# First block's layers as whole float32 products, weight splits made later and weight conversion moved behind each step's work

## Chip, cores and metric

The kernel runs on one core of a Trainium2 chip. The metric is the device time of one execution in microseconds (us). Before the change the median of three runs is 1035.82 us, the lowest 1035.16 us.

## What is computed

An attention-like recurrence (wkv) over 768 steps, for 4 sequences and 8 heads of 48 channels, gives 3072 tokens of 384 values. Two layers follow:

```python
h = x @ w_in                                  # 384 -> 2048
x = (h * clip(h + 3, 0, 6) / 6) @ w_out       # 2048 -> 384
xn = x / sqrt(mean(x * x) + 1e-6) * rms_g
g = xn @ w_gate                               # 384 -> 1536
x = (g / (1 + exp(-g)) * (xn @ w_val)) @ w_out2   # 1536 -> 384
```

Inputs are float32; the weights of the two layers come as 64-bit words (float64) and are turned into float32 on the core.

## The kernel before

**Blocks.** The 768 steps are cut in six chunks (c = 0 to 5) of 128 steps; a chunk of all four sequences is a block of 512 tokens. Attention is worked in 24 jobs (chunk, sequence). The first layer takes block after block, and attention jobs of later blocks run between its matmuls. Then comes the second layer (`gps`, `vps` and `o` products), block after block, in which only matmuls and their follow-up remain.

**Steps.** The first layer is a list of 101 steps, each for one slice f (of 16) of the 2048 hidden values. A step (`ff1`) makes `hps` in three k-tiles (`emit_h`), then relu6 on ScalarE and VectorE (`emit_act`), then the split of the result; two steps later `ff2` adds the slice's part into three accumulators `o` (`emit_out`). In block 0 the first five slices are done in two halves of 256 tokens (steps 0 to 4 and 5 to 9), since the jobs of sequences 2 and 3 are not ready yet; steps 10 to 20 take 512 tokens each. Block 1 has eight slices in halves, from step 21.

**Products.** A float32 operand is split in two float32r parts, high and low; a product of a 128x128 weight tile is three matmuls (`PASS`: high-high, high-low, low-high). Hence nine matmuls for a step's `hps` and nine for its `o`. Splits: weights in `Weight.parts` (high on ScalarE, low on GpSimd), hidden values in `emit_split` (the same), attention output in `split_y0` (ScalarE, VectorE) for block 0.

**Weights.** Each weight tile (128x768, 64 bits each) is loaded to `raw`, then `scale` (ScalarE, tile `mag`, one buffer), `bits` (three VectorE instructions L143, L144, L146 into tile `x`), then `parts`. The 16 tiles of the first layer are converted during block 0, the 18 of the second one (`wb`) during block 5 and the first eight steps of the second layer. What a step does before its matmuls, between and behind them is in the lists `before`, `between` and `behind`; `pin` fixes each engine's order to that of the code. Every engine works its own instructions in that order.

**Norm.** When a block's last `o` is done, `Norm` copies the three accumulators away (two on ScalarE, L378, one on VectorE, L376); the next block's first `o` waits for these copies. The rest of the norm is spread over later steps.

Of the kernel before, what the change touches and what calls it, by code (L numbers as in the profile page):

```python
# [9 lines left out]
F32 = mybir.dt.float32  # L10
# [12 lines left out]
DM = H * D  # L23
# [6 lines left out]
NB = 3 * F2 // 2  # L30
NX = 6
NE = 10
# [4 lines left out]
def kernel(  # L37
# [84 lines left out]


    class Weight:
        def __init__(self, src, dst):
            self.src, self.dst = src, dst

# [8 lines left out]
        def scale(self):  # L136
            self.mag = st_p.tile([128, 2 * DM], F32, tag="mag", name="mag", bufs=1)
# [20 lines left out]
    class Job:  # L158
# [172 lines left out]

        def split_y0(self):
            xt = self.xt()
            nc.scalar.activation(out=xt[:, :, 0, :], in_=self.yps, func=AF.Copy)
            nc.vector.tensor_tensor(
                out=xt[:, :, 1, :], in0=self.yps, in1=xt[:, :, 0, :].bitcast(F32), op=ALU.subtract)

# [7 lines left out]

    def emit_act(ps, n):
        a = rg_p.tile([128, n], F32, tag="a", name="a", bufs=2)
        nc.scalar.activation(out=a, in_=ps, func=AF.Relu, scale=1.0 / 6.0, bias=half)  # L348
        nc.vector.scalar_tensor_tensor(out=a, in0=a, scalar=1.0, in1=ps, op0=ALU.min, op1=ALU.mult)  # L349
        return a  # L350

# [5 lines left out]

    def emit_out(acc, slot, g, first, last, cols, **kw):
        for m in range(KT):
            for j, (l, r) in enumerate(PASS):  # L360
                nc.tensor.matmul(  # L361
                    acc[m][:, cols], slot[:, l, m * 128:(m + 1) * 128], g[:, r, :],
                    start=(first and j == 0), stop=(last and j == 2), **kw)

# [4 lines left out]
    class Norm:  # L369
# [41 lines left out]
    jobs = [Job(c, b) for c in range(NC_) for b in range(B)]  # L411
    wa = [Weight(wa_d[f], None) for f in range(F1)]
    whole, halves = slice(0, TOK), (slice(0, HT), slice(HT, TOK))
# [65 lines left out]
    def ff1(c, f, cols):  # L479
        n = cols.stop - cols.start  # L480
        ps = ps_h.tile([128, n], F32, tag="h", name="hps")
        emit_h(wpair[f][:, 0], xts[c][:, :, :, cols], ps)
        a = emit_act(ps, n)
        g = emit_split(a, n)
        todo.append(lambda: ff2(c, f, cols, g))

    def ff2(c, f, cols, g):
        nonlocal acc
        lagged = LAGS[c] > 0
        if f == 0 and cols.start == 0:  # L490
            acc = new_acc()
            if lagged:
                for m in range(KT):
                    nc.tensor.matmul(
                        acc[m], zero, wpair[0].rearrange("p a l n -> p (a l n)")[:, 0:TOK], start=True, stop=False)
        last = f == F1 - 1
        emit_out(acc, wpair[f][:, 1], g, f == 0 and not lagged, last, cols)
        if last:
            norms[c] = Norm(c, acc)
# [17 lines left out]

    j0.load("w", "rk")
    j1.load("w")
    for t, s in ((iperm, iperm_d), (mask, mask_d)):  # L520
        nc.sync.dma_start(out=t, in_=s)
    nc.vector.memset(uc, 0.0)
    for i in range(2):
        nc.sync.dma_start(
            out=uc[64 * i:64 * i + D, :, i], in_=u_d.rearrange("o (p i d) -> i d (o p)", p=NP, i=2)[i])
    j1.load("rk")
    j0.load("v")
# [17 lines left out]
    for t in st_all:  # L545
        nc.gpsimd.memset(t, 0.0)
    nc.scalar.activation(out=zero, in_=st_all[3][:, 0:128], func=AF.Copy)
    for f in range(W1):
        wa[f].dst = wpair[f]
    run((j0.scans, j0.pairs, j0.pe_bonus, j0.muls, j0.fill, j0.pe_a, j1.scans, j1.pairs, j1.pe_bonus, j1.muls))  # L550
    run((j0.choose, j1.fill, j1.pe_a, j0.pe_y0, wa[0].scale, wa[0].bits, j1.choose, j1.pe_y0))
    run((j0.split_y0, wa[0].parts, wa[1].scale, wa[1].bits, j1.split_y0, j2.scans, wa[1].parts))
    pin()


    for n, (c, f, cols) in enumerate(steps):
# [8 lines left out]
        if n == first[NC_ - 1]:  # L565
            actx.close()
            st_p = pool(ctx, "st2", 2, side="left", reuse_waits="tile")
            b_p = pool(ctx, "bp", 2, side="left", reuse_waits="tile")
# [3 lines left out]
            wb = [Weight(wb_d[i], extra[i] if i < NX else wpair[i - NX]) for i in range(NB)]  # L572
            wb[0].load()
            wb[1].load()
        run(before[n])
        if c == NC_ - 1:
# [16 lines left out]
        run(behind[n])  # L593
        pin()
# [26 lines left out]
    for c in range(NC_):  # L621
        for f in range(F2):
            if c == 0:
                if f < NB - NE:
                    wb[NE + f].scale()
# [17 lines left out]
            if len(todo) > 2:  # L643
                todo.pop(0)()
            if c == 0 and 2 <= f < 2 + len(NORM):
                x = NORM[f - 2]
                getattr(norms[NC_ - 1], x[0])(*x[1:])
            if c + 1 < NC_:
# [91 lines left out]
```

## Time and profile before

| what | value |
|---|---|
| median of three runs | 1035.82 us |
| the profiled execution, its own time | 1035.39 us |
| its span, first to last instruction | 1033.6 us |
| TensorE (PE) busy | 972.1 us, 94% |
| VectorE (DVE) busy | 482.4 us, 47% |
| ScalarE (ACT) busy | 405.5 us, 39% |
| GpSimd (POOL) busy | 441.8 us, 43% |
| loads to `raw` (768 KB each), issue to landing, median | 4.3 us |
| mean granted TensorE clock | 0.969 of full speed |

The profile is of one execution. Each engine works through its own instructions in order; where an instruction waits, the profile says for which other engine. Shares of the whole span hide that stretches differ, so the stretches are read one by one. The span of a PE row is modelled at its end; the distance between starts is what a stream of matmuls costs. PEld rows are the weight loads that go with the matmuls. PEclk is the granted clock of TensorE as a share of 2.4 GHz; 0.5 is the lower of its two levels, 1.2 GHz.

### The profile page before, as it was taken

What the parts mean: (1) busy time and instruction counts of PE and PEld (TensorE: products, weight loads), DVE (VectorE), ACT (ScalarE), POOL (GpSimd) and SP (SyncE); (2) the same over time, 40 slices, a digit from 0 to 9 for tenths busy, and PEclk for the clock granted to TensorE, in tenths of its full rate; (3) what the DMA queues carried; (4) which work ended last, traced back from release to release, by engine and by line L of the source; (5) the groups of instructions that cost most, each with busy time, mean ns of one, the idle gap of its engine ahead of it and who ended that gap; (6) DMA issues with size and microseconds to landing.
All of it is one profiled execution on the core that took longest, in us unless ns stands there. A gap on an engine that the chain in (4) does not pass through costs nothing.

```text
span 1033.6 us, 14038 instructions
## 1 busy us (share of the span) xinstructions
PE 972.1 (94%) x5517; PEld 804.5 (78%) x5517; DVE 482.4 (47%) x597; ACT 405.5 (39%) x774; POOL 441.8 (43%) x361
## 2 busy tenths in 40 slices
PE   5588799899999999999998899999999999999998
PEld 4587588778888888877776677888888888888887
DVE  7858865564457556655378666412112112112111
ACT  3365365544544544454454535322222212222222
POOL 1346675455465665664375555411122112211121
PEclk9589889899999999999999989999999999999999
DMA  8236422434222422330333332010100100100000
GB/s 313 90 123 224 151 90 83 141 112 140 77 77 84 168 75 77 124 129 8 130 131 101 135 97 88 37 56 1 59 2 1 62 1 1 62 1 1 31 1 30
DMA packets 32417, 85.65 MB, mean 83 GB/s; under 512 B 5728, under 2 KB 12768, under 8 KB 32352
## 3 DMA queue, kind: packets, MB, share of 16 engines
q1 hardware_dynamic: 32352, 84.76, 23.7%
q8 instruction: 43, 0.70, 0.3%
q14 instruction: 22, 0.18, 0.0%
HBM read 71.37 MB, written 9.44 MB: 78 GB/s over the span
## 4 chain that ended last, share of the span: by engine, by line
PE 73%; DVE 10%; issue 6%; ACT 5%; POOL 2%; DMA 2%; SPq 1%; ACTq 0%; POOLq 0%; DVEq 0%
PE o L361 26%; PE hps L342 13%; PE gps L342 13%; PE vps L342 13%; DVE x L144 3%; PE aps L251 2%; PE yps L293 2%; DVE x L146 2%; DVE x L143 2%; ACT a L348 1%; POOL wpair L152 1%; DVE a L349 1%; PE yps L287 1%; ACT a L232 1%; DVE w L174 1%
## 5 line engine op out<-in xcount | busy, mean ns | idle before, releaser
L361 PE MATMUL o<-g,wpair 128*128 128x512 f32 (+1 forms) x1422 | 330.5, 377 | 1.8 <-DVE x L376 1.7
L361 PEld LDWEIGHTS o<-g,wpair 128*128 128x128 f32 x1422 | 252.6, 191 | 50.2 <-DVE x L376 2.1
L342 PE MATMUL hps<-xt,wpair 128*128 128x512 f32 (+1 forms) x981 | 221.5, 371 | 15.8 <-DVE a L349 8.7
L355 POOL TENSOR_TENSOR g<-a,g 128x512 fp32r<-128x512 f32 (+1 forms) x109 | 141.1, 1295 | 204.8 <-ACT g L354 194.4
L355 POOL TENSOR_TENSOR g<-s,g 128x512 fp32r<-128x512 f32 x72 | 95.8, 1330 | 299.1 <-ACT g L354 298.7
L342 PEld LDWEIGHTS hps<-xt,wpair 128*128 128x128 f32 x981 | 173.1, 193 | 49.5 <-DVE a L349 11.3
L636 DVE TENSOR_TENSOR s<-s,vps 128x512 f32<-128x512 f32 x72 | 49.5, 687 | 309.2 <-PE vps L342 289.8
L349 DVE SCALAR_TENSOR_TENSOR a<-a,hps 128x512 f32<-128x512 f32 (+1 forms) x109 | 67.5, 619 | 170.1 <-ACT a L348 170.0
L348 ACT ACTIVATE a<-hps,half 128x512 f32<-128x512 f32 (+1 forms) x109 | 68.6, 629 | 98.6 <-PE hps L342 93.9
L342 PE MATMUL gps<-xt,wpair 128*128 128x512 f32 x432 | 105.9, 389 | 0.0
L342 PE MATMUL vps<-xt,wpair 128*128 128x512 f32 x432 | 105.7, 389 | 0.0
L354 ACT ACTIVATE g<-a 128x512 fp32r<-128x512 f32 (+1 forms) x109 | 63.4, 581 | 107.6 <-DVE a L349 106.1
L354 ACT ACTIVATE g<-s 128x512 fp32r<-128x512 f32 x72 | 45.5, 632 | 146.1 <-DVE s L636 146.1
L633 ACT ACTIVATE s<-gps 128x512 f32<-128x512 f32 x72 | 42.9, 596 | 150.3 <-PE gps L342 150.3
L342 PEld LDWEIGHTS gps<-xt,wpair 128*128 128x128 f32 x432 | 81.0, 188 | 17.2 <-ACT s L633 0.5
L342 PEld LDWEIGHTS vps<-xt,wpair 128*128 128x128 f32 x432 | 81.1, 188 | 16.8
L152 POOL TENSOR_TENSOR wpair<-x,wpair 128x768 fp32r<-128x768 f32 x28 | 56.6, 2021 | 67.7 <-ACT wpair L151 67.7
L174 DVE TENSOR_TENSOR_SCAN w<-w,dd 128x520 f32<-128x520 f32 x48 | 80.0, 1666 | 4.5 <-DMA w<-in_dram 2.8
L361 PE MATMUL o<-g,bpair 128*128 128x512 f32 x216 | 55.2, 400 | 5.9 <-ACT x L378 3.8
L232 ACT ACTIVATE a<-iperm,cb 128x128 f32<-128x128 f32 x192 | 58.5, 387 | 0.1
L342 PE MATMUL gps<-xt,bpair 128*128 128x512 f32 x216 | 54.6, 398 | 0.2 <-ACT s L633 0.2
L138 ACT ACTIVATE mag<-raw 128x768 f32<-128x768 f32 x34 | 30.5, 897 | 59.1 <-issue 29.5
(75 smaller groups left out, 967.5 us busy)
## 6 DMA issues: line engine op xcount, KB each, us to landing
raw<-in_dram SPq DMA_DIRECT2D x34, 768.0 KB, 4.3
w<-in_dram SPq DMA_DIRECT2D x24, 520.0 KB, 3.8
rk<-in_dram SPq DMA_DIRECT2D x24, 512.0 KB, 4.5
rks<-in_dram SPq DMA_DIRECT2D x20, 384.0 KB, 4.7
v<-in_dram SPq DMA_DIRECT2D x24, 256.0 KB, 4.8
xn<-x SPq DMA_DIRECT2D x6, 768.0 KB, 4.3
xraw<-xn SPq DMA_DIRECT2D x6, 768.0 KB, 5.1
out_dram<-osb SPq DMA_DIRECT2D x15, 256.0 KB, 2.5
```

Of the source, the lines that this page charges most:

```text
L144: nc.vector.scalar_tensor_tensor(out=x, in0=high, scalar=0x80000000, in1=x, op0=ALU.bitwise_and, op1=ALU.bitwise_or)
L152: nc.gpsimd.tensor_tensor(out=self.dst[:, :, 1, :], in0=self.x, in1=self.dst[:, :, 0, :].bitcast(F32), op=ALU.subtract)
L174: nc.vector.tensor_tensor_scan(out=x, data0=x, data1=dd.rearrange("p a h j -> p (a h j)"), initial=0.0, op0=ALU.mult, op1=ALU.add)
L232: nc.scalar.activation(out=self.head(h), in_=iperm, func=AF.Copy, scale=self.cb[:, h, :])
L342: nc.tensor.matmul(ps, slot[:, l, k * 128:(k + 1) * 128], xt[:, k, r, :], start=(k == 0 and j == 0), stop=(k == KT - 1 and j == 2))
L348: nc.scalar.activation(out=a, in_=ps, func=AF.Relu, scale=1.0 / 6.0, bias=half)
L349: nc.vector.scalar_tensor_tensor(out=a, in0=a, scalar=1.0, in1=ps, op0=ALU.min, op1=ALU.mult)
L354: nc.scalar.activation(out=g[:, 0, :], in_=a, func=AF.Copy)
L355: nc.gpsimd.tensor_tensor(out=g[:, 1, :], in0=a, in1=g[:, 0, :].bitcast(F32), op=ALU.subtract)
L361: nc.tensor.matmul(acc[m][:, cols], slot[:, l, m * 128:(m + 1) * 128], g[:, r, :], start=(first and j == 0), stop=(last and j == 2), **kw)
L633: nc.scalar.activation(out=s, in_=gp, func=AF.Silu)
L636: nc.vector.tensor_tensor(out=s, in0=s, in1=vp, op=ALU.mult)
```

## The change

**Block 0 in whole float32.** In block 0 only, a product is one float32 matmul of unsplit operands (`emit_h_f32`, `emit_out_f32`): three instructions for a step's `hps` and three for its `o`. Hidden values and attention output of block 0 are no longer split (`copy_y0` copies alone). Converted weights stay whole: VectorE's `x` is copied by a DMA into the place of the low part of `wpair` (393 KB each, on SP's queue, ahead of the next `raw` load), and the matmuls of slices 2 and up read it there; slices 0 and 1 read `x` in their first half.

**Splits later.** The 16 weight tiles of the first layer are split at the start of steps 11 to 26, in place; block 1 uses the parts from step 21 on. The low part, for both layers' weights, is now made on VectorE (`nc.vector`) and no longer on GpSimd.

**Conversion behind the work.** In block 5 and at the start of the second layer, `scale` and `bits` stand behind the step's accumulator products, the norm's piece and the norm's copies; `mag` gets a second buffer there, `bpair` has five tiles instead of six.

**Small edits.** The three `o` clears with `zero` (L494) fall away in blocks 0 and 1; the `uc` loads stand right behind the first load; a `Silu` of one column is put behind the norm of block 4.

```diff
-NX = 6
+NX = 5
...
         def bits(self):
             low, high = self.words()
-            x = st_p.tile([128, 2 * DM], U32, tag="x", name="x")
+            x = st_p.tile([128, 2 * DM], U32, tag="x", name="x", bufs=2 if self.pairs else 3)
...
+            if not self.pairs:
+                nc.sync.dma_start(
+                    out=self.dst[:, :, 1, :].bitcast(U32), in_=x.rearrange("p (a n) -> p a n", a=2))
+                if not self.near:
+                    self.x = self.dst[:, :, 1, :].bitcast(F32)
...
         def parts(self):
             nc.scalar.activation(out=self.dst[:, :, 0, :], in_=self.x, func=AF.Copy)
-            nc.gpsimd.tensor_tensor(
+            nc.vector.tensor_tensor(
                 out=self.dst[:, :, 1, :], in0=self.x, in1=self.dst[:, :, 0, :].bitcast(F32), op=ALU.subtract)
...
+    def emit_h_f32(slot, xt, ps):
+        for k in range(KT):
+            nc.tensor.matmul(
+                ps, slot[:, k * 128:(k + 1) * 128], xt[:, k, 0, :].bitcast(F32),
+                start=(k == 0), stop=(k == KT - 1))
...
-    begun = {f: f - 2 for f in range(2, W1 + 1)} | {8: 7} | {f: f + 1 for f in range(9, F1)}
+    begun = {f: f - 2 for f in range(2, W1)} | {7: 7, 8: 8} | {f: f + 1 for f in range(9, F1)}
     for f, n in begun.items():
         before[n] += [wa[f].scale]
         behind[n] += [wa[f].bits]
-        before[n + 1 if f < 5 else n + 2] += [wa[f].parts]
...
+    for f in range(F1):
+        before[f + 11] += [wa[f].parts]
...
-            if f in begun2:
-                wb[begun2[f]].scale()
             if f - 2 in begun2:
                 wb[begun2[f - 2]].parts()
         ff1(c, f, cols)
         run(between[n])
+        while len(todo) > 2:
+            todo.pop(0)()
+        if c == NC_ - 1 and f in begun2:
+            wb[begun2[f]].scale()
+        run(behind[n])
         if c == NC_ - 1 and f in begun2:
             wb[begun2[f]].bits()
             wb[begun2[f] + 2].load()
-        while len(todo) > 2:
-            todo.pop(0)()
-        run(behind[n])
```

VectorE's order at the start, ahead of step 0, from the mask copies of job 1 to the first scan of job 2 (`x`: weight tile 1; L335: the low part of the attention output), before:

```order
L257 COPY_PREDICATED a<-mask,aps 128x512 x2
L335 TENSOR_TENSOR xt<-yps,xt 128x3x128
L143 TENSOR_SCALAR x<-raw 128x768
L144 SCALAR_TENSOR_TENSOR x<-raw,x 128x768
L146 SCALAR_TENSOR_TENSOR x<-mag,x 128x768
L335 TENSOR_TENSOR xt<-yps,xt 128x3x128
L179 MEMSET dd 128x8
L174 SCALAR_TENSOR_TENSOR w<-w,dd 128x520
```

The same place in the changed kernel (line numbers are 2 to 12 higher):

```order
L265 COPY_PREDICATED a<-mask,aps 128x512 x2
L145 TENSOR_SCALAR x<-raw 128x768
L146 SCALAR_TENSOR_TENSOR x<-raw,x 128x768
L148 SCALAR_TENSOR_TENSOR x<-mag,x 128x768
L187 MEMSET dd 128x8
L182 SCALAR_TENSOR_TENSOR w<-w,dd 128x520
```

The two low parts of the attention output are gone from the queue; the two later ones, of jobs 2 and 3, go likewise.

VectorE's order in block 0 from the relu6 of step 10 (first row) to that of step 11 (last row), before:

```order
L349 SCALAR_TENSOR_TENSOR a<-a,hps 128x512
L143 TENSOR_SCALAR x<-raw 128x768
L144 SCALAR_TENSOR_TENSOR x<-raw,x 128x768
L146 SCALAR_TENSOR_TENSOR x<-mag,x 128x768
L179 MEMSET dd 128x8
L174 SCALAR_TENSOR_TENSOR w<-w,dd 128x520
L182 RECIPROCAL dd<-w 128x8
L174 SCALAR_TENSOR_TENSOR w<-w,dd 128x520
L349 SCALAR_TENSOR_TENSOR a<-a,hps 128x512
```

The same place in the changed kernel (`wpair_115` is the first weight tile, split in place):

```order
L365 SCALAR_TENSOR_TENSOR g<-g,hps 128x512
L145 TENSOR_SCALAR x<-raw 128x768
L146 SCALAR_TENSOR_TENSOR x<-raw,x 128x768
L148 SCALAR_TENSOR_TENSOR x<-mag,x 128x768
L187 MEMSET dd 128x8
L182 SCALAR_TENSOR_TENSOR w<-w,dd 128x520
L190 RECIPROCAL dd<-w 128x8
L182 SCALAR_TENSOR_TENSOR w<-w,dd 128x520
L160 TENSOR_TENSOR wpair_115<-wpair_115 128x2x384
L365 SCALAR_TENSOR_TENSOR g<-g,hps 128x512
```

One subtraction of 768 columns is added ahead of the relu6; so it is in each of the steps 11 to 26.

VectorE's order at the start of the second layer, from the product `s` of its step 1 to that of step 2 (`x_5421<-o` is the norm's copy that frees an accumulator), before:

```order
L636 TENSOR_TENSOR s<-s,vps 128x512
L143 TENSOR_SCALAR x<-raw 128x768
L144 SCALAR_TENSOR_TENSOR x<-raw,x 128x768
L146 SCALAR_TENSOR_TENSOR x<-mag,x 128x768
L376 COPY x_5421<-o_4874 128x512
L636 TENSOR_TENSOR s<-s,vps 128x512
```

The same place in the changed kernel:

```order
L663 TENSOR_TENSOR s<-s,vps 128x512
L392 COPY x_5103<-o_4563 128x512
L145 TENSOR_SCALAR x<-raw 128x768
L146 SCALAR_TENSOR_TENSOR x<-raw,x 128x768
L148 SCALAR_TENSOR_TENSOR x<-mag,x 128x768
L160 TENSOR_TENSOR wpair_120<-x,wpair_120 128x2x384
L663 TENSOR_TENSOR s<-s,vps 128x512
```

The norm's copy stands ahead of the three conversion instructions, and a subtraction of 768 columns is added behind them.

## Rows read from the trace of the kernel before

**Rows 1.** Stretches: bounds, length, busy us by engine (instructions), PEclk, DMA share, GB/s.

```profile
0.00:57.06 57.06, 33.81 (x235) 29.53 (x236) 43.83 (x62) 23.46 (x57) 12.70 (x17) 0.77 0.50 183
57.06:161.35 104.29, 90.56 (x675) 76.61 (x675) 72.55 (x86) 54.30 (x104) 68.57 (x53) 0.92 0.42 147
161.35:507.14 345.79, 337.05 (x2384) 279.84 (x2383) 196.26 (x269) 166.89 (x356) 193.67 (x181) 0.99 0.31 104
507.14:607.89 100.75, 88.82 (x364) 69.51 (x363) 72.73 (x71) 50.62 (x77) 58.57 (x34) 0.95 0.35 118
607.89:1033.60 425.71, 421.84 (x1867) 348.99 (x1865) 97.01 (x112) 110.24 (x181) 108.25 (x78) 1.00 0.08 28
```

**Rows 2.** PE's waits, 57 to 161 us: total us, times, longest.

```profile
PE hps L342 <- DVE a L349: 4.6, 2, 4.0
```

**Rows 3.** PE's waits, 507 to 608 us.

```profile
PE hps L342 <- DVE a L349: 4.1, 4, 1.3
PE o L361 <- ACT x L378: 3.8, 1, 3.8
PE o L361 <- DVE x L376: 3.7, 2, 2.0
```

**Rows 4.** Weight loads in order: start, us, nine matmuls each, first 256 then 512 columns.

```profile
75.69 1.15 PEld L342 LDWEIGHTS hps<-xt,wpair 128*128 128x128 f32 x9
76.77 1.15 PEld L361 LDWEIGHTS o<-g,wpair 128*128 128x128 f32 x9
...
503.06 2.00 PEld L342 LDWEIGHTS hps<-xt,wpair 128*128 128x128 f32 x9
505.10 2.00 PEld L361 LDWEIGHTS o<-g,wpair 128*128 128x128 f32 x9
```

**Rows 5.** Lines of matmuls: count, ns min/median/max (first two), busy and mean (last).

```profile
L239 PE MATMUL ktp<-ident,rk x80: 272/273/473, 53.0 to 404.0; 128*128 128x128 f32 x80
L361 PE MATMUL o<-g,wpair x1422: 277/389/774, 55.1 to 1029.6; 128*128 128x512 f32 x146, 128*128 128x256 f32 x32
L251 PE MATMUL aps<-rk 48*128 48x128 f32 x384 | 34.3, 329 | 6.0 <-DVE rk L197 2.8 <-issue 2.6 <-PE cps L220 0.6
```

**Rows 6.** VectorE in order at the start: start, us, instruction, idle before and releaser.

```profile
21.09 0.56 DVE L335 TENSOR_TENSOR xt<-yps,xt 128x384 fp32r<-128x384 f32 x1 [0.79 <-ACT xt L334]
...
22.15 2.45 DVE L144 SCALAR_TENSOR_TENSOR x<-raw,x 128x768 uint32<-128x768 uint32 x1
24.70 0.96 DVE L146 SCALAR_TENSOR_TENSOR x<-mag,x 128x768 uint32<-128x768 uint32 x1
25.58 0.55 DVE L335 TENSOR_TENSOR xt<-yps,xt 128x384 fp32r<-128x384 f32 x1
...
26.19 1.24 DVE L174 TENSOR_TENSOR_SCAN w<-w,dd 128x520 f32<-128x520 f32 x1
...
27.71 2.42 DVE L174 TENSOR_TENSOR_SCAN w<-w,dd 128x520 f32<-128x520 f32 x1
...
36.81 2.43 DVE L174 TENSOR_TENSOR_SCAN w<-w,dd 128x520 f32<-128x520 f32 x1
...
44.28 0.56 DVE L335 TENSOR_TENSOR xt<-yps,xt 128x384 fp32r<-128x384 f32 x1 [3.52 <-ACT xt L334]
```

**Rows 7.** VectorE's groups, 507 to 608 us: busy us, mean ns, idle before.

```profile
L146 DVE SCALAR_TENSOR_TENSOR x<-mag,x 128x768 uint32<-128x768 uint32 x13 | 20.2, 1557 | 0.5
L349 DVE SCALAR_TENSOR_TENSOR a<-a,hps 128x512 f32<-128x512 f32 x15 | 10.2, 682 | 18.8 <-ACT a L348 18.8
L636 DVE TENSOR_TENSOR s<-s,vps 128x512 f32<-128x512 f32 x4 | 2.8, 688 | 9.1 <-ACT s L633 9.1
```

**Rows 8.** Order of time: a float32 subtraction of 512 columns on VectorE; a conversion on ScalarE.

```profile
542.37 2.33 DVE L513 TENSOR_TENSOR xt<-xraw,xt 128x512 fp32r<-128x512 f32 x1
...
553.25 0.69 DVE L513 TENSOR_TENSOR xt<-xraw,xt 128x512 fp32r<-128x512 f32 x1
...
589.91 0.89 ACT L138 ACTIVATE mag<-raw 128x768 f32<-128x768 f32 x1 [2.85 <-DVE x L146]
```

More of the change, by code (lines that the diff above doesn't have):

```diff
@@ L136, in scale @@
         def scale(self):
[L137 removed]
+            self.mag = st_p.tile([128, 2 * DM], F32, tag="mag", name="mag", bufs=mag_bufs)
             nc.scalar.activation(out=self.mag, in_=self.words()[1].bitcast(F32), func=AF.Copy, scale=2.0 ** -112)
@@ L344, in emit_h, with emit_out_f32, emit_act @@
                     start=(k == 0 and j == 0), stop=(k == KT - 1 and j == 2))
-    def emit_act(ps, n):
-        a = rg_p.tile([128, n], F32, tag="a", name="a", bufs=2)
+    def emit_h_f32(slot, xt, ps):
[3 more added lines that the diff above has]
+                start=(k == 0), stop=(k == KT - 1))
+    def emit_out_f32(acc, slot, g, first, cols):
+        for m in range(KT):
+            nc.tensor.matmul(
+                acc[m][:, cols], slot[:, m * 128:(m + 1) * 128], g,
+                start=first, stop=True, skip_group_check=not first)
+    def emit_act(ps, n, a):
         nc.scalar.activation(out=a, in_=ps, func=AF.Relu, scale=1.0 / 6.0, bias=half)
         nc.vector.scalar_tensor_tensor(out=a, in0=a, scalar=1.0, in1=ps, op0=ALU.min, op1=ALU.mult)
-        return a
     def emit_split(a, n, p=None):
@@ L356, in emit_split, with emit_out @@
         return g
-    def emit_out(acc, slot, g, first, last, cols, **kw):
+    def emit_out(acc, slot, g, first, last, cols, parts=False):
         for m in range(KT):
@@ L362, in emit_out @@
                     acc[m][:, cols], slot[:, l, m * 128:(m + 1) * 128], g[:, r, :],
-                    start=(first and j == 0), stop=(last and j == 2), **kw)
+                    start=(first and j == 0), stop=(parts or last and j == 2),
+                    skip_group_check=parts and not (first and j == 0))
     def new_acc():
@@ L411 @@
     jobs = [Job(c, b) for c in range(NC_) for b in range(B)]
-    wa = [Weight(wa_d[f], None) for f in range(F1)]
+    wa = [Weight(wa_d[f], None, False) for f in range(F1)]
     whole, halves = slice(0, TOK), (slice(0, HT), slice(HT, TOK))
@@ L481, in ff1, with ff2 @@
         ps = ps_h.tile([128, n], F32, tag="h", name="hps")
[L482 to L487, printed above, removed]
+        if c == 0:
+            if cols.start:
+                wa[f].x = wpair[f][:, :, 1, :].bitcast(F32)
+            emit_h_f32(wa[f].x[:, 0], xts[c][:, :, :, cols], ps)
+            g = rg_p.tile([128, n], F32, tag="g", name="g")
+            emit_act(ps, n, g)
+        else:
+            emit_h(wpair[f][:, 0], xts[c][:, :, :, cols], ps)
+            a = rg_p.tile([128, n], F32, tag="a", name="a", bufs=2)
+            emit_act(ps, n, a)
+            g = emit_split(a, n)
+        x = wa[f].x[:, 1] if c == 0 else wpair[f][:, 1]
+        todo.append(lambda: ff2(c, f, cols, g, x))
+    def ff2(c, f, cols, g, x):
         nonlocal acc
-        lagged = LAGS[c] > 0
-        if f == 0 and cols.start == 0:
+        first, last = f == 0 and cols.start == 0, f == F1 - 1
+        if first:
             acc = new_acc()
[L492 to L497, printed above, removed]
+        if c == 0:
+            emit_out_f32(acc, x, g, first, cols)
+        else:
+            emit_out(acc, x, g, first, last, cols, LAGS[c] > 0)
         if last:
@@ L515, in load_x @@
         return part
[L518 to L521, printed above, removed]
+    j0.load("w")
     nc.vector.memset(uc, 0.0)
@@ L525 @@
             out=uc[64 * i:64 * i + D, :, i], in_=u_d.rearrange("o (p i d) -> i d (o p)", p=NP, i=2)[i])
+    j0.load("rk")
+    j1.load("w")
+    for t, s in ((iperm, iperm_d), (mask, mask_d)):
+        nc.sync.dma_start(out=t, in_=s)
     j1.load("rk")
@@ L546 @@
         nc.gpsimd.memset(t, 0.0)
-    nc.scalar.activation(out=zero, in_=st_all[3][:, 0:128], func=AF.Copy)
     for f in range(W1):
         wa[f].dst = wpair[f]
+        wa[f].near = f < 2
     run((j0.scans, j0.pairs, j0.pe_bonus, j0.muls, j0.fill, j0.pe_a, j1.scans, j1.pairs, j1.pe_bonus, j1.muls))
     run((j0.choose, j1.fill, j1.pe_a, j0.pe_y0, wa[0].scale, wa[0].bits, j1.choose, j1.pe_y0))
-    run((j0.split_y0, wa[0].parts, wa[1].scale, wa[1].bits, j1.split_y0, j2.scans, wa[1].parts))
+    run((j0.copy_y0, wa[1].scale, wa[1].bits, j1.copy_y0, j2.scans))
     pin()
@@ L571 @@
             extra += [bw_p.tile([128, 2, 2, DM], F32R, name=f"bpair{i}") for i in range(NX)]
-            wb = [Weight(wb_d[i], extra[i] if i < NX else wpair[i - NX]) for i in range(NB)]
+            wb = [Weight(wb_d[i], extra[i] if i < NX else wpair[i - NX], True) for i in range(NB)]
             wb[0].load()
@@ L638 @@
             todo.append(lambda c=c, f=f, g=g: out2(c, f, g))
+            if len(todo) > 2:
+                todo.pop(0)()
+            if c == 0 and f < NB - NE:
+                wb[NE + f].scale()
+            if c == 0 and 2 <= f < 2 + len(NORM):
+                x = NORM[f - 2]
+                getattr(norms[NC_ - 1], x[0])(*x[1:])
             if c == 0 and f < NB - NE:
```

30 lines of the change are left out of this document (12 added, 18 removed).

## Prediction

> **What bounds the kernel now.** I read the stretches first [rows 1]. From 607.89 us to the end, and from 161.35 to 507.14, TensorE (PE) is busy nearly all the time at a clock of 0.99 to 1.00: the products set the pace there, and the change leaves them alone. Two stretches lose time. From step 3's first product to the end of block 0's last accumulator product (57.06 to 161.35) PE is idle for 104.29 - 90.56 = 13.7 us, and the mean clock of 0.92 costs another 0.08 x 104.29 = 8.3 us: a loss of 22.0. In the 100.75 us around the border of the layers the same sum gives 11.9 + 0.05 x 100.75 = 16.9. Ahead of step 3 PE has little to do (33.81 of 57.06) and VectorE is the busy one (43.83).
>
> Then I read who is late. In block 0 the largest wait of PE is a product that needs a buffer which VectorE's relu6 has not freed yet [rows 2]; at the border it is the same wait, and the accumulators that the norm's copies have not freed [rows 3]. So both losses lie behind VectorE's queue, in which the weight conversion stands ahead of the relu6 and of those copies.
>
> **The float32 products.** A nine-matmul product costs 1.08 us at 256 columns and 2.04 us at 512, start to start [rows 4]. No whole float32 matmul of this size is in the trace. What is there: the float32 score matmuls, eight in the program for each of 24 jobs, leave 384 records, so one is two records [rows 5]; and a float32 record of 128 columns lasts 272 ns, as long as a float32r record of 256 columns (277, the shortest; 389 is 512 columns) [rows 5]. A float32 column thus takes the time of two. A whole product is 2 records x 2 = 4 units against 3 before, a factor of 4/3: 1.44 us for 256 columns, 2.72 for 512. The lower bound is two records at the float32r rate, a factor of 2/3. I take 4/3, since 272 sits on 277 and not on the time that 128 columns would have. The Trainium skill, FP8 and Floating Point Precision, section TensorE Precision Notes, says that true float32 is four passes through the array; by that too the factor is 4/3, and no run here shows it yet.
>
> From step 3 on, block 0 has 22 products of 512 columns (steps 10 to 20, two each) and 16 of 256 (7 `hps`, 9 `o`): 22 x 0.68 + 16 x 0.36 = 20.7 us more for PE.
>
> **The start.** VectorE's queue loses, up to the third weight tile [rows 6]: the low parts of the attention output and the waits ahead of them (0.79 + 0.56, 0.55, 3.52 + 0.56), and the stretching of three instructions that ran beside GpSimd's weight subtractions: 2.45 where the same kind of instruction takes 0.96, and two scans of 2.42 and 2.43 where 1.24 is normal. With no split in block 0 GpSimd has nothing to do there. Sum: 9.8 us. PE's two `hps` and one `o` product in that chain grow by 0.36 each, at the lower clock double: 2.2 us. Step 3 begins 7.6 us sooner. The new DMA of each weight tile is hidden: a tile is used a full step or more after its conversion, and the `raw` loads, twice its size, land in 4.3 us (table of the profile); if that cover were gone at steps 2 to 4 it would cost 2 us each. The SP queue gets 16 such transfers ahead of `raw` loads that had to wait for the same conversion anyway. The `uc` loads gain next to nothing, since job 1 hangs on VectorE.
>
> **Block 0's loss.** VectorE gets a subtraction of 768 columns at each of the steps 11 to 20 of this stretch. For 512 columns one took 0.69 alone and 2.33 in company [rows 8]; scaled to 768 that is 1.0 and 3.5. I take 1.0, since in block 0 GpSimd keeps only the jobs' small work. VectorE is busy 72.55 us there [rows 1]; ten subtractions make 82.6, even if no conversion shortens, while PE's own work grows from 104.29 - 22.0 = 82.3 to 103.0. So VectorE no longer sets the pace on the mean. The worst steps (11, 15, 19) hold two scans (2 x 1.24), three conversion instructions (0.96 at most), the subtraction and the relu6 (0.68): some 7 us against PE's 5.4 (two products of 2.72). Being 1.6 us late at each is covered by the two `hps` buffers and the two steps between a slice's `hps` and its `o`. I put 2 us of stall here, 2 on the state chains of steps 3 to 6, in which ScalarE's part stays, and 2 for GpSimd's job work that stretches VectorE: the loss falls from 22.0 to 6, with bounds 2 and 24 (no better than before).
>
> So by the end of block 0: 7.6 - 20.7 + 16.0 = 2.9 us gained. The three clears of block 1, matmuls of 512 columns at 2.04/9 each, give 0.7. The six subtractions that fall in block 1 (1.0 to 3.5 each) meet half steps of 2.2 us and a stretch that loses 8.7 us already [rows 1]; I charge 0.6, bounds -4 and +6.
>
> **The border.** VectorE is busy 72.73 of 100.75 us and stands 18.8 + 9.1 = 27.9 us waiting for ScalarE's relu or silu [rows 7]. ScalarE in turn stood behind `scale`, which waits for VectorE's last conversion instruction since `mag` has one buffer [rows 8]: a loop. With the second buffer and the conversion at the step's end it opens, and the norm's copies (3.8 + 3.7 [rows 3]) go ahead of the conversion. VectorE's work stays about the same: the conversion instruction of 1557 ns mean [rows 7], 0.96 alone, shortens when GpSimd's subtractions go, and 13 subtractions come. Without company that is some 70 us of work for 82 us of products (40 at 2.04, less idle and lost clock). I let 5 of 16.9 remain: a gain of 11.9, bounds 3 and 17. The moved table load is in that.
>
> **Sum.** 2.9 + 0.7 - 0.6 + 11.9 = 14.9. The profiled execution took 1035.39 us (span 1033.6 and 1.8 around it), 0.4 under the median of 1035.82: 1035.4 - 14.9 = 1020.5, say 1020.
>
> **Rivals.**
> - *Clean.* Block 0 loses only 2 to 3, block 1 catches up 5 of its lost time since no half clock follows, the border keeps 1: 1035.4 - (2.9 + 3.5 + 0.7 + 5 + 16) = 1007. For it: VectorE's idle time in [rows 7] is larger than what is added. Against: the border's steps are uneven. Chance 0.22.
> - *The border keeps its loss.* The conversion merely moves and VectorE is again late, now at the relu6: gain there 3, total 1035.4 - (2.9 + 0.7 - 0.6 + 3) = 1029. For it: VectorE's 72.73 busy us [rows 1] do not shrink if the subtractions run in company. Chance 0.16.
> - *Slower.* VectorE's new subtractions run in company at 3.5 us, so block 0's loss does not fall. It decides at a loss of 22 + 7.6 - 20.7 = 9 for the start alone and near 21 for the whole kernel; at 24 the start loses 15.1, and with 8 of such stretching in block 1 and only 3 won at the border the time is 1035.4 + 15.1 - 0.7 + 8 - 3 = 1055. For it: 2.33 in [rows 8]; against: GpSimd's splits, its company, leave block 0. Chance 0.08. The Trainium skill, SBUF - State Buffer, section Who interferes with whom, says that a VectorE instruction with two SBUF inputs contends with GpSimd reads; the subtractions are of that kind, and the stretched rows at 22 us agree.
> - *Float32 at the lower bound.* Factor 2/3: PE's work in block 0 falls by 20.7 instead, VectorE paces it, and half of the difference of 41.4 is won: 1020 - 21 = 999. Against: the record lengths of [rows 5]. Chance 0.06.
>
> The forecast itself has 0.48. Its own range is 1011 to 1029.
>
> **How the numbers follow.** About 2% is what a measurement of this kernel tells from no change: under 1015 or over 1057. Faster: *clean* nearly whole (0.20), *lower bound* 0.06, and a sixth of the forecast (0.08): 0.34. Slower: half of its rival's upper part, 0.03. Within: 0.63. Leaving out the float32 rival, most of the slower one and the ends of the rest, the range is 1003 to 1037.
>
> **What would show it.** The float32 products of steps 10 to 20 at 2.7 us start to start (1.4 would be the lower bound). Step 3 near 49 us, block 0's last `o` ended near 157. VectorE's weight instructions in block 0 near 0.96. At the border, no wait of `o` for the norm's copies, and VectorE's wait for ScalarE well under 28. I am wrong if PE stands idle over 10 us between step 3 and the end of block 0, or if block 1's half steps wait for VectorE.

## The result and the profile after

The changed kernel takes 1025.16 us (median of four runs, 1019.44 to 1027.49) against 1035.82 for the kernel before, run beside it: 10.7 us less, a ratio of 0.989, 95% interval 0.9867 to 0.9913. One run of the kernel before, of 3332.09 us, is left out; with it the median would be 1036.78. The forecast was 1020 us, with a range of 1003 to 1037 and most of the chance on "within 2%". The number came out close; the sum behind it did not come out term by term, and that is what the rest is about.

The profiled execution of after took 1027.49 us (span 1025.7), the slowest of the four, so stages are compared here and totals by the medians. Its stretches, cut at the same events as [rows 1] (step 3's first product; end of block 0; the same product of block 5; the first `gps` with a `wpair` weight), with the columns of [rows 1]:

```profile
0.00:44.63 44.63, 29.08 (x220) 24.38 (x221) 33.82 (x55) 18.86 (x49) 1.91 (x12) 0.92 0.76 269
44.63:159.21 114.58, 103.02 (x561) 62.56 (x560) 73.07 (x103) 45.16 (x87) 19.41 (x21) 0.96 0.50 175
159.21:511.03 351.82, 339.77 (x2381) 279.06 (x2379) 200.61 (x273) 168.91 (x360) 193.30 (x180) 0.99 0.30 102
511.03:595.34 84.31, 84.13 (x363) 67.60 (x362) 76.44 (x81) 49.07 (x76) 34.34 (x21) 1.00 0.41 138
595.34:1025.70 430.36, 426.32 (x1867) 348.82 (x1865) 100.33 (x119) 111.89 (x183) 97.42 (x72) 1.00 0.08 29
```

| stretch | before [rows 1] | after | gained | forecast |
|---|---|---|---|---|
| start, to step 3 | 57.06 | 44.63 | 12.4 | 7.6 |
| step 3 to the end of block 0 | 104.29 | 114.58 | -10.3 | -4.7 |
| rest of blocks 1 to 5 ahead of the border | 345.79 | 351.82 | -6.0 | 0.1 |
| border of the layers | 100.75 | 84.31 | 16.4 | 11.9 |
| second layer | 425.71 | 430.36 | -4.6 | 0 |

Two losses were not in the forecast at all: the two long stretches in which the products set the pace, and which the change was said to leave alone, lost 10.6 us between them.

**The border** is clean. The answer to [rows 3] is a single line of waits of PE, and VectorE's wait for ScalarE's relu and silu of [rows 7], 18.8 + 9.1 us, is 3.5, all for the relu (first fence PE's waits, second VectorE's, both 507 to 608 us):

```profile
PE hps L347 <- DVE a L365: 0.2, 1, 0.2
```

```profile
DVE a L365 <- ACT a L364: 3.5, 1, 3.5
```

VectorE is busier than before (76.44 us of 84.31) and still never late: 0.18 us of PE's time is idle in this stretch.

**The start.** The end of the chain to step 3, PE in order of time, kernel before (first) and after:

```profile
53.72 1.63 PE L494 MATMUL o<-wpair,zero 128*128 128x512 f32 x3
55.14 2.12 PE L361 MATMUL o<-g,wpair 128*128 128x256 f32 x9
57.06 1.13 PE L342 MATMUL hps<-xt,wpair 128*128 128x256 f32 x6
```

```profile
43.33 1.46 PE L359 MATMUL o<-g,x 128*128 128x256 f32 x6
44.63 1.46 PE L353 MATMUL hps<-xt,wpair 128*128 128x256 f32 x6
```

The clears with `zero` cost 1.42 us here (53.72 to 55.14); the `o` product behind them takes 1.30 us instead of 1.92, although it is float32 now: the granted clock is 1.00 from 43.33 to 44.63 us, and was 0.50, the lower level, from 55.14 to 57.06 before.

**Float32 products.** Start to start, PE, 512 columns:

```profile
109.24 2.74 PE L359 MATMUL o<-g,wpair 128*128 128x512 f32 x6
111.81 2.74 PE L353 MATMUL hps<-xt,wpair 128*128 128x512 f32 x6
114.39 1.88 PE L359 MATMUL o<-g,wpair 128*128 128x512 f32 x4
```

2.575 us, not 2.72; at 256 columns 1.295 (weight loads at 64.29, 65.58), not 1.44. Against 2.04 and 1.08 for nine float32r matmuls [rows 4] that is a factor of 1.26 and 1.20.

**Block 0's loss.** Idle 114.58 - 103.02 = 11.6, and 0.04 x 114.58 = 4.6 of clock: 16.1, where 6 was forecast. What PE waited for from 44.63 to 159.21, then what ScalarE and VectorE waited for there (first line of PE's and ScalarE's, second of VectorE's; the same wait of `mag` for `raw` was 2.8 us before):

```profile
PE yps L295 <- DVE a L265: 6.7, 2, 3.4
```

```profile
ACT mag L140 <- DMA raw<-in_dram: 29.3, 7, 8.3
```

```profile
DVE wpair L160 <- ACT wpair L159: 13.3, 7, 4.7
```

One of these chains, in order of time. ScalarE:

```profile
120.65 0.91 ACT L140 ACTIVATE mag<-raw 128x768 f32<-128x768 f32 x1 [8.32 <-DMA raw<-in_dram]
121.47 0.83 ACT L159 ACTIVATE wpair<-wpair 128x768 fp32r<-128x768 f32 x1
122.20 0.67 ACT L364 ACTIVATE g<-hps,half 128x512 f32<-128x512 f32 x1
```

and VectorE behind it:

```profile
122.33 0.96 DVE L160 TENSOR_TENSOR wpair<-wpair 128x768 fp32r<-128x768 f32 x1 [4.66 <-ACT wpair L159]
123.20 0.68 DVE L365 SCALAR_TENSOR_TENSOR g<-g,hps 128x512 f32<-128x512 f32 x1
...
128.61 1.32 DVE L265 COPY_PREDICATED a<-mask,aps 128x512 f32<-128x512 uint32 x2
```

`mag` waits 8.3 us for a late `raw` tile; the high copy (L159) and the relu (L364) stand behind it on ScalarE; VectorE's subtraction (L160) waits for the high copy; relu6 (L365) and the mask copy (L265), for which PE's `yps` waits, stand behind the subtraction. The subtraction itself takes 0.96 us, as forecast (1.0), and no conversion instruction is stretched much (means of 0.61, 1.02 and 0.97 us).

### The profile page after: what moved, and what is told of

It is laid out like the page before. It is cut to its first block, busy times and chain, and to the rows that moved or that the text cites. A ratio compares the mean times of both kernels' runs of the same rounds, so it can differ in the third digit from the quotient of the medians.

```text
span 1025.7 us, 13752 instructions
## 1 busy us (share of the span) xinstructions
PE 982.3 (96%) x5385; PEld 782.4 (76%) x5385; DVE 484.3 (47%) x627; ACT 393.9 (38%) x753; POOL 346.4 (34%) x306
## 4 chain that ended last, share of the span: by engine, by line
PE 79%; DVE 9%; ACT 4%; DMA 4%; issue 3%; SPq 1%; POOL 0%; ACTq 0%; DVEq 0%; POOLq 0%
PE o L376 27%; PE gps L347 14%; PE vps L347 14%; PE hps L347 12%; DMA raw<-in_dram 3%; PE aps L259 2%; PE yps L301 2%; DVE x L146 2%; PE o L359 2%; PE yps L295 1%; DVE x L148 1%; PE hps L353 1%; DVE a L365 1%; PE ktp L247 1%; DVE w L182 1%
## 5 line engine op out<-in xcount | busy, mean ns | idle before, releaser
L376 PE MATMUL o<-g,wpair 128*128 128x512 f32 (+1 forms) x1287 | 306.1, 382 | 0.0
L376 PEld LDWEIGHTS o<-g,wpair 128*128 128x128 f32 x1287 | 230.4, 189 | 48.8 <-issue 0.7
L347 PE MATMUL hps<-xt,wpair 128*128 128x512 f32 (+1 forms) x792 | 182.9, 375 | 3.4 <-POOL xt L324 2.1
L370 POOL TENSOR_TENSOR g<-a,g 128x512 fp32r<-128x512 f32 (+1 forms) x88 | 113.9, 1295 | 196.7 <-ACT g L369 185.4
L347 PEld LDWEIGHTS hps<-xt,wpair 128*128 128x128 f32 x792 | 139.7, 188 | 34.2 <-POOL xt L324 2.3
L347 PE MATMUL vps<-xt,wpair 128*128 128x512 f32 x486 | 120.4, 392 | 0.0
L365 DVE SCALAR_TENSOR_TENSOR a<-a,hps 128x512 f32<-128x512 f32 (+1 forms) x88 | 55.7, 633 | 129.3 <-ACT a L364 129.2
L364 ACT ACTIVATE a<-hps,half 128x512 f32<-128x512 f32 (+1 forms) x88 | 56.6, 643 | 96.1 <-PE hps L347 89.5
L209 POOL TENSOR_TENSOR rks<-rks 128x384 f32<-128x384 f32 x20 | 29.2, 1460 | 64.7 <-DMA rks<-in_dram 64.7
L347 PEld LDWEIGHTS gps<-xt,bpair 128*128 128x128 f32 x216 | 40.5, 188 | 8.8
```

What stands on the lines that cost most here:

```text
L209: nc.gpsimd.tensor_tensor(out=x, in0=x, in1=self.rks[:, 1, :], op=ALU.mult)
L347: nc.tensor.matmul(ps, slot[:, l, k * 128:(k + 1) * 128], xt[:, k, r, :], start=(k == 0 and j == 0), stop=(k == KT - 1 and j == 2))
L370: nc.gpsimd.tensor_tensor(out=g[:, 1, :], in0=a, in1=g[:, 0, :].bitcast(F32), op=ALU.subtract)
L376: nc.tensor.matmul(acc[m][:, cols], slot[:, l, m * 128:(m + 1) * 128], g[:, r, :], start=(first and j == 0), stop=(parts or last and j == ...
```

## Experiments

Each run was timed beside the kernel before (medians 1035.5 to 1036.0); the ratio is to that one. Lines are those of the kernel after.

### The two halves of the change

**e1, the border's edits alone**, in the kernel before (the diff's hunks on `mag_bufs`, `scale` and `bits` behind the step, `NX = 5`, the early `Silu`; the subtraction on VectorE for `pairs` only).

> The kernel before with the border's part of the change alone: conversion behind each step's products and choices, two buffers for mag, five bpair tiles, the subtraction of those weights on VectorE, the early Silu. If the change's two parts add up as the two traces suggest, the border (100.75 us before, 84.31 us after) gives 16.4 us and nothing else moves: 1036.8 - 16.4 = 1020 us, and the last stage keeps its 425.7 us. If the 4.6 us that the last stage lost in the trace of after belong to the border's edits (five tiles, moved buffers), the sum is 16.4 - 4.6 = 11.8: 1025 us, with the nine products of the last stage at 2.10 us. If my own step for the border (11.9 us) is the truth and the rest of the 16.4 came from block 0, 1025 us with 4 to 5 us of waits left at the border.

**e2, block 0's edits alone**: those hunks of the kernel after undone.

> The kernel after with the border's part undone: float32 products in block 0, whole weights copied by DMA, split ten steps later on VectorE, the earlier start. The stages of the trace of after say: start -12.4, block 0 +10.3, blocks 1 to 5 +6.0, so +3.9 us: 1041 us. If the 6.0 us of blocks 1 to 5 are the execution's and not the kernel's, 1035 us. If block 0 was a gain as I predicted (2.9 us), 1034 us.

e1: 1027.92 us, ratio 0.9922 (0.9898 to 0.9947). e2: 1040.9, ratio 1.0046 (1.0028 to 1.0064). By stages e1's border is the one of after (84.34 us), but its second layer takes 430.12 us, not 425.7. And the halves do not add: -7.7 and +5.2 make -2.5, the whole made -10.7. It is as if each half held a cost of about 8 us that the whole holds once.

### ScalarE's and VectorE's order in block 0

**e3, `mag` behind the relu:**

```diff
-        before[n] += [wa[f].scale]
-        behind[n] += [wa[f].bits]
+        behind[n] += [wa[f].scale, wa[f].bits]
```

> The kernel after with one thing moved: in block 0 ScalarE's mag stands behind the step's hi copy and relu instead of ahead of them, directly ahead of the three VectorE conversions. Theory 1 (block 0's remaining loss of about 16 us is the late raw load: ScalarE waits 27.5 us in mag with the hi copy and the relu queued behind it): mag's waits no longer stand ahead of a relu, TensorE's losses in block 0 halve, 5 to 9 us less than after: 1016 to 1020 us. Theory 2 (VectorE is loaded by the added subtractions and is itself the late engine): within 2 us of after, 1023 to 1027 us.

**e4, block 0's subtraction on GpSimd:**

```diff
-            nc.vector.tensor_tensor(
+            (nc.vector if self.pairs else nc.gpsimd).tensor_tensor(
                 out=self.dst[:, :, 1, :], in0=self.x, ...
```

> The kernel after with block 0's weight subtractions on GpSimd again (VectorE keeps those of the border). Theory 2 (VectorE's added subtractions, 0.96 us each, and its wait for the hi copies make relu6 late): 5 us or more less than after, 1020 us or below. Theory 1 (the relu itself is late, behind mag): relu6 still waits for the relu, so within 3 us of after, 1022 to 1028 us. Theory 3 (a GpSimd subtraction beside VectorE's conversions slows both): 3 to 10 us more than after, 1028 to 1035 us, with VectorE's L146 and L148 well over their 0.96 us.

e3: 1020.37 us, ratio 0.9849 (0.9815 to 0.9882), just above what theory 1 gave; e4: 1021.10, ratio 0.9856 (0.9827 to 0.9885). Start and block 0, e3 and then e4:

```profile
0.00:48.73 48.73, 30.34 (x220) 25.03 (x221) 36.13 (x59) 19.26 (x49) 1.91 (x12) 0.84 0.70 246
48.73:152.55 103.82, 98.85 (x561) 60.26 (x561) 71.02 (x99) 45.85 (x86) 20.27 (x21) 0.99 0.55 193
```

```profile
0.00:43.63 43.63, 28.38 (x220) 23.51 (x221) 33.73 (x55) 18.81 (x49) 1.91 (x12) 0.88 0.77 275
43.63:152.65 109.02, 100.22 (x561) 60.49 (x560) 68.38 (x91) 45.29 (x87) 43.78 (x33) 0.98 0.52 183
```

Both end block 0 some 6.6 us sooner than after (152.55 and 152.65 against 159.21), in different ways. e3 cuts block 0 from 114.58 to 103.82 and pays 4.1 in the start, where VectorE's conversion now waits 5.9 us for `mag` instead of 2.0. e4 leaves `mag` where it is; the wait for the high copy moves from VectorE to GpSimd, which has nothing else to do:

```profile
L160 POOL TENSOR_TENSOR wpair<-wpair 128x768 fp32r<-128x768 f32 x12 | 24.0, 2000 | 24.4 <-ACT wpair L159 24.4
```

So it is one chain with two links, and cutting either frees it. e4 alone could not tell VectorE's load from its wait (1021.1 lies between the two expectations); e3, which leaves VectorE its subtractions, and e8 below, which takes them away on top of e3's edit and gains nothing, speak for the wait. Work on GpSimd beside it has a price, but a small one: VectorE's scans of block 0 average 1.65 us in e4, 1.39 in after. (The Trainium skill, SBUF — State Buffer, section Who interferes with whom, says that a VectorE instruction with two SBUF inputs contends with GpSimd's reads; a scan is one, and the 0.26 us agree with it.)

### Where the last stage's 4.6 us went

The products of the second layer are the same instructions as before. Their weight loads in after, first with weights in `wpair` 4 and 2, then in `wpair` 10, 10, 8 and 11 (which tile a load reads follows from the program's order):

```profile
609.62 2.00 PEld L347 LDWEIGHTS vps<-xt,wpair 128*128 128x128 f32 x9
611.66 2.00 PEld L376 LDWEIGHTS o<-g,wpair 128*128 128x128 f32 x9
...
632.92 2.06 PEld L347 LDWEIGHTS gps<-xt,wpair 128*128 128x128 f32 x9
635.02 2.05 PEld L347 LDWEIGHTS vps<-xt,wpair 128*128 128x128 f32 x9
637.12 2.05 PEld L376 LDWEIGHTS o<-g,wpair 128*128 128x128 f32 x9
639.22 2.05 PEld L347 LDWEIGHTS gps<-xt,wpair 128*128 128x128 f32 x9
```

The first take 2.04 us start to start, as in [rows 4]; the second 2.10, with `xt` as with `g`, at a granted clock of 1.00 in both. What differs is the place in SBUF. In the built programs `wpair` 7 to 15 are allocated from the right end and never move: they begin at byte 224 in a block of 256. The tiles on the left that products read (`wpair` 0 to 6, `xt`, `g`, `bpair`) began at 224 too in the kernel before; in after they begin at 0, since `zero` went (512 bytes) and `spare` came (32 with its padding). e1 added `spare`, e2 did both: they share the shift.

**e5, after with the 32 bytes given back:**

```diff
-    eps = const.tile([128, 1], F32, name="eps")
-    spare = const.tile([128, 1], F32, name="spare")
+    two = const.tile([128, 2], F32, name="two")
+    eps, spare = two[:, 0:1], two[:, 1:2]
```

> The kernel after with one change in placement: spare and eps share one tile, so that everything allocated behind them on the left side (wpair 0 to 6, xt, g, bpair) begins 32 bytes lower, at 224 in its block of 256 bytes, as it did in the kernel before and as wpair 7 to 15 on the right side do in all kernels. Theory P (placement: a float32r product whose xt or g and whose weights stand at different offsets streams at 2.10 us per nine matmuls instead of 2.04): the last stage gives back 4.6 us, blocks 1 to 5 some 5, so 1025 - 9.5 = 1015.5 us, and every product of the last stage is at 2.04. Rival (the 2.10 comes with five bpair tiles, or from the neighbours' traffic): within 2 us of the kernel after.

**e6, the kernel before with `spare` (and a memset of it) added**, nothing else.

> The kernel before with one thing added: a 4-byte tile (and its memset) ahead of gain, which moves the left side's tiles from offset 224 to 0 as in the kernel after, while wpair 7 to 15 stay at 224. Theory P: products with wpair 7 to 15 go from 2.04 to 2.10 us, some 10 to 11 us more: 1046 us. Rival (the change's own traffic or tile count): within 2 us of the kernel before.

e5: 1014.4 us, ratio 0.9792 (0.9758 to 0.9826), 10.8 less than after. e6: 1043.6, ratio 1.0068 (1.0046 to 1.0091), 8.1 more than before, somewhat less than theory P gave. e5's weight loads with `wpair` 10 and 8, now 2.04 us start to start, and its stretches:

```profile
627.24 2.00 PEld L347 LDWEIGHTS vps<-xt,wpair 128*128 128x128 f32 x9
629.28 2.00 PEld L376 LDWEIGHTS o<-g,wpair 128*128 128x128 f32 x9
631.32 2.00 PEld L347 LDWEIGHTS gps<-xt,wpair 128*128 128x128 f32 x9
```

```profile
0.00:42.62 42.62, 28.27 (x220) 23.78 (x221) 34.06 (x56) 19.11 (x49) 1.91 (x12) 0.92 0.79 282
42.62:155.97 113.35, 102.98 (x561) 63.03 (x560) 73.22 (x103) 44.77 (x87) 19.87 (x21) 0.95 0.50 176
155.97:503.91 347.94, 336.56 (x2380) 279.49 (x2379) 200.55 (x273) 168.71 (x360) 192.93 (x180) 0.99 0.31 103
503.91:587.99 84.08, 83.32 (x364) 67.64 (x363) 76.20 (x81) 49.13 (x76) 34.25 (x21) 1.00 0.40 137
587.99:1013.30 425.31, 421.28 (x1867) 349.12 (x1865) 100.36 (x120) 111.68 (x183) 97.09 (x72) 1.00 0.08 29
```

The last stage is back at 425.31, and the stage before the border gained 3.9. In e6 it is the other way round:

```profile
611.77:1042.10 430.33, 425.66 (x1867) 348.69 (x1865) 97.00 (x112) 111.10 (x182) 109.52 (x79) 1.00 0.08 28
```

The size fits: of the 36 weight pieces that a block's products of the second layer read, 12 lie in `wpair` 7 to 12; that makes 72 products in six blocks, and 0.06 us each is 4.3; products with weights on the left that stand next to these are up to 0.04 us longer, 0.8 in all. The stage lost 430.36 - 425.31 = 5.1. The float32 products of block 0 show nothing of it: 2.57 us with weights on the right in after (140.10 to 142.67) as in e5 (136.85 to 139.43). Moving one 4-byte constant thus costs this kernel 8 to 11 us, about as much as the whole change brought.

**e10, e5 with 64 bytes of padding behind `gain`** (left side at byte 32).

> Run e5 with 64 bytes of padding behind gain: the left side's tiles stand at 32 in their 256 bytes, wpair 7 to 15 at 224, so the two sides agree in their place within 64 bytes and differ within 128 and 256. If the place within 64 bytes decides: 1014 us as run e5, products of the last stage at 2.04. If the place within 128 or 256 decides: 1024 us, products with wpair 7 to 15 at 2.10.

1020.23 us, ratio 0.9847 (0.9832 to 0.9861): neither of the two. Products with weights on the right take 2.06 us, with `xt` as with `g` (628.14 to 634.32); the one at 626.10, with `wpair` 6 on the left, takes 2.04:

```profile
626.10 2.00 PEld L377 LDWEIGHTS o<-g,wpair 128*128 128x128 f32 x9
628.14 2.02 PEld L348 LDWEIGHTS gps<-xt,wpair 128*128 128x128 f32 x9
630.20 2.02 PEld L348 LDWEIGHTS vps<-xt,wpair 128*128 128x128 f32 x9
632.26 2.02 PEld L377 LDWEIGHTS o<-g,wpair 128*128 128x128 f32 x9
634.32 2.02 PEld L348 LDWEIGHTS gps<-xt,wpair 128*128 128x128 f32 x9
```

The place within 64 bytes is therefore not the rule, or not alone: agreeing there, the products still lose a third of it. Against e5 the run is 5.8 us longer. The last stage lost 1.5 of that, 72 products at 0.02; the 3.1 lost in the stretch of blocks 1 to 5 are only partly this. What the rule is stays open.

**e11, e1 with the 32 bytes given back**, as in e5.

> Run e1 (the border's part alone) with the 32 bytes given back, as in run e5. Theory P: 1027.9 - 8 to 10 = 1018 to 1020 us, that is 16 to 17 under the kernel before, all of it at the border. Against run e5 it gives what block 0's part is worth in the same placement: 3 to 6 us gained. If the border's gain needs block 0's part (shared buffers, state of the queues), 1023 us or more.

1016.59 us, ratio 0.9813 (0.9798 to 0.9827), a little under what theory P gave. The border's part alone is worth 19.1 us in this placement and 1043.6 - 1027.9 = 15.7 in the other. Block 0's part is then worth 1016.6 - 1014.4 = 2.2 (e5) and 1043.6 - 1040.9 = 2.7 (e2 against e6); their ratio intervals overlap, so this is a small gain at the edge of what these runs resolve.

### Towards a better kernel

**e7, e5 with e3's edit; e8, e7 with e4's edit.**

> Run e5 and run e3 together: the 32 bytes given back, and mag behind the relu in block 0. If the two add: 1020.4 - 9.5 = 1011 us. If the placement's loss is hidden wherever TensorE waits anyway, 1013 to 1015.

> Run e7 with block 0's weight subtractions on GpSimd too (run e4). In the trace of run e4 the subtractions left VectorE free for the relu6; with mag already behind the relu there is less to win: 1 to 3 us under run e7, 1008 to 1010. If GpSimd's subtractions lengthen VectorE's conversions (1.6 us in company in the kernel before), 0 to 3 us above run e7.

e7: 1013.16 us, ratio 0.9771 (0.974 to 0.9801); e8: 1013.30, ratio 0.9771 (0.9744 to 0.9798). In e7's trace step 3 begins at 49.23 us and block 0 takes 103.51 us: against e5 block 0 wins 9.8 and the start loses 6.6 of it. The edit helps in the one place and hurts in the other.

**e9, the edit from step 5 on only:**

```diff
-        before[n] += [wa[f].scale]
+        (before if n < 5 else behind)[n] += [wa[f].scale]
```

> Run e5 with mag behind the relu from step 5 on, and ahead of it (as in the kernel after) in steps 0 to 4. Theory 1 (late raw loads held up the relu in the middle of block 0, while in the start mag ahead of the relu is right, since there TensorE waits for the conversion): the start of run e5 (42.6 us to step 3) with block 0 of run e7 (103.5 us): 1014.4 - 9.8 = 1004.6, and some of it may be given back in block 1: 1004 to 1009 us. Rival (what was lost in the start of run e7 is lost later here, since the raw loads and VectorE set block 0's pace): 1012 to 1014 us, as run e7.

1006.88 us, ratio 0.9711 (0.9695 to 0.9727): 2.9% under the kernel before and 18 us under the kernel after. Both halves are there:

```profile
0.00:45.12 45.12, 28.38 (x220) 23.51 (x221) 33.82 (x55) 18.78 (x49) 1.90 (x12) 0.89 0.74 266
45.12:149.86 104.74, 98.20 (x561) 59.83 (x560) 73.39 (x103) 45.84 (x87) 20.28 (x21) 1.00 0.55 191
```

`mag` still waits 16.1 us for `raw` in this block; with no relu behind it, PE is idle 6.5 us instead of 10.4 and the granted clock is 1.00.

**e12, e9 with the split behind the step too:**

```diff
-        before[f + 11] += [wa[f].parts]
+        behind[f + 11] += [wa[f].parts]
```

> Run e9 with the split of block 0's weights (ScalarE's hi copy, VectorE's subtraction) behind the step's products and choices as well, instead of ahead of them. Theory 1b (in block 1 ScalarE's hi copy stands ahead of the fill and the relu, and VectorE's subtraction behind it delays the mask choice that yps waits for): the yps waits between block 0's end and 220 us (some 7.6 us in run e9) shrink to 3 or less, and the stretch of blocks 1 to 5 falls from 349.2 towards the 342.9 of run e11: 1001 to 1004 us. Rival (the subtraction's place does not matter, the half-rate clock at block 1's start comes from the jobs alone): 1005 to 1009 us, as run e9.

1011.55 us, ratio 0.9771 (0.9754 to 0.9787): 4.7 us slower than e9, which neither theory gave. PE's waits from block 0's end to 222 us, e9 and then e12:

```profile
PE yps L295 <- DVE a L265: 5.3, 2, 4.4
PE yps L295 <- POOL g L370: 2.3, 1, 2.3
PE hps L347 <- POOL xt L324: 2.2, 1, 2.2
```

```profile
PE yps L295 <- POOL g L370: 3.2, 2, 2.2
PE aps L259 <- issue: 3.2, 2, 2.9
PE hps L347 <- POOL xt L324: 2.5, 1, 2.5
PE hps L347 <- ACT xt L323: 2.5, 1, 2.5
```

The 4.4 us wait for the mask copy did go, and 2.1 us were won in block 0; but block 1's half steps only waited elsewhere, for the attention output's parts and in `aps`, and the stretch got longer:

```profile
149.86:222.00 72.14, 60.91 (x570) 56.13 (x569) 45.86 (x70) 37.15 (x87) 36.27 (x42) 0.91 0.35 118
```

```profile
147.78:222.00 74.22, 60.53 (x561) 55.79 (x560) 45.91 (x70) 37.78 (x88) 34.83 (x41) 0.86 0.35 114
```

e12 idles 13.7 us there and has 0.86 of the clock, e9 11.2 and 0.91. Removing the longest wait of this stretch gained nothing, since others grew in its place.

## Why the prediction came out, step by step

The traces of before and e5 stand in the same placement, so they show the change itself; the last column has the shifted placement besides. Each column is one execution: the start, in the same order of instructions, took 42.6 to 45.1 us in the traces of after, e2, e4, e5, e9, e10 and e12, so a difference of 2 us in a stage is not told from none.

| term | forecast | measured, placement as before (e5) | after |
|---|---|---|---|
| start | 7.6 | 14.4 | 12.4 |
| float32 products | -20.7 | -15.2 | -15.2 |
| block 0's loss cut from 22.0 | 16.0 | 6.0 (to 16.0) | 5.9 (to 16.1) |
| blocks 1 to 5 ahead of the border | 0.1 | -2.2 | -6.0 |
| border | 11.9 | 16.7 | 16.4 |
| second layer | 0 | 0.4 | -4.6 |
| sum of the stages | 14.9 | 20.3 | 7.9 |

(The products and the loss together leave 1.0 us of block 0 in after unexplained; in e5 they meet its 9.1.) The forecast's 14.9 and the 10.7 measured between the medians are near each other because a gain some 5 us larger than forecast met a loss of 8 to 11 us that the forecast did not contain. The sign was right, and the mechanism of the border and the start; the nearness of 1020 and 1025 is partly luck.

- **Float32 products: direction right, size off.** Two records per matmul held, but 5.5 us too much was charged. 22 x 0.535 + 16 x 0.215 = 15.2. The step that failed is taking records of equal length for equal streaming. Per float32 record 0.429 us at 512 columns and 0.216 at 256: twice the columns is twice the time. A float32r record is 0.227 and 0.120: 0.107 for 256 columns more and 0.013 besides. Nine such fixed shares go, six nearly free ones come. By the Trainium skill, FP8 and Floating Point Precision, section TensorE Precision Notes, true float32 is four passes through the array; one matmul's two records take 2 x 0.213 per 256 columns, four times 0.107: it holds for the streaming part. By it alone the factor is 4/3; the fixed part lowers it.
- **The start: undercounted by 5 to 7 us.** The chain was read rightly, but the clears (1.42), the stretched `rk` product of 2.91 us (1.29 normal) behind the last counted row and a third conversion (1.37 for 0.96) were missed, and the 2.2 us charged for the longer products arose only in part: the third `hps` product took 2.2 us instead of 1.3 (from 38.70 us, granted clock 0.63), but the `o` product 0.6 less than before, at 1.00.
- **Block 0's loss: wrong**, by the forecast's own mark (more than 10 us idle: 11.6). Its step said a subtraction of 1.0 us fits VectorE's mean load; it does (73.07 of 114.58 us). The step that failed is its list of 6 us of stalls (2, 2 and 2), which has no late `raw` in it: `mag` waited 29.3 us for `raw`, 2.8 before. The working took the SP queue's new transfers as free, "ahead of `raw` loads that had to wait for the same conversion anyway", and that is not quite so. A `raw` tile is free after `mag` and VectorE's second conversion instruction, and before the change SP waited for that (41.9 us in block 0, 8 times); the transfer ahead of the load waits for the third (55.9 us, 10 times). The loads that follow take 5.5 us to land, 4.4 before. The late `raw` reached PE through ScalarE's order, of which the working spoke only at the border. e3, e7 and e9 show that link. What makes `raw` late stays open: no run takes the transfers away, and the jobs' loads and the stores of `y` stand in the same queue (the load behind the wait of 8.3 us was issued at 112.82, right after eight such stores, three such loads and a transfer).
- **Blocks 1 to 5: within the bounds.** A gain of 0.1 was forecast, with bounds of -4 and +6 on a loss of 0.6; -2.2 without the placement, of the size that executions differ by (the kernel before took 345.79 us here, e11 342.90 with the same instructions). The mark "block 1's half steps wait for VectorE" was met: one `yps` wait of 4.4 us in after, which the profile puts down to GpSimd's `g` and which ended together with VectorE's mask copy. e12 shows that it is not one cause.
- **The border: right, and better than forecast.** 5 us of loss were kept for uneven steps; 0.2 remained. e1 and e11 show it independent of block 0. VectorE's conversion did not shorten as said (L148 1.52 us mean, 1557 ns in [rows 7]), although GpSimd's work there fell from 58.57 to 34.34 us; why stays open. PE did not wait for it: in the new order the relu6 and the copies stand ahead of it.
- **The placement: missing.** The working set the long stretches at no change because their instructions do not change. Nothing in it looked at where the tiles come to lie.

Of the rivals, *clean* was nearest for the border and the start, and without the shift of 32 bytes the kernel would have stood between it and the forecast. *The border keeps its loss* fell with its 0.2 us of idle time, *slower* and *float32 at the lower bound* with subtractions of 0.96 us and products of 2.575.

## What to carry over

An engine's in-order queue passes a late load on to everything behind it: put the instruction that waits for a DMA behind the one that feeds TensorE, but only where TensorE waits for the latter (e3 lost in the start what e9 kept). When the halves of a change don't add up, look for what both carry, and compare the rate of an untouched inner stream first: here a 3% longer product at an unchanged clock pointed to placement, not order. Removing the longest wait need not pay: in e12 PE waited as long elsewhere.

## What was not expected of the hardware

- Nine float32r matmuls of 512 columns take 2.04, 2.06 or 2.10 us at the same granted clock, depending on where the moving tile (`xt` or `g`) and the weights begin in SBUF: both at byte 224 in 256 (e5), or both at 0 (after, `wpair` 0 to 6), 2.04; moving tile at 32 and weights at 224 (e10), 2.06; moving tile at 0 and weights at 224 (after, `wpair` 7 to 12), 2.10. Float32 products show no such difference (2.57 in after and e5). Worth 8.1 to 11.3 us of this kernel (e6, e11 against e1).
- A float32 matmul is two records of 0.429 us for 512 columns; it costs 1.26 times the three float32r matmuls that it replaces, 1.20 at 256 columns.
- A subtraction of 768 columns takes 2.00 us on GpSimd (e4) and 0.96 on VectorE.
